# Recurrent attention and a two-layer network: the second layer of nine units by seven half-width products, decay sums in a state bank, new engine orders

## The chip, the cores and the metric

The kernel runs on one core of one Trainium2 chip. The metric is device time in microseconds for one launch; the runs of a kernel are given by their median.

## The reference

A gated recurrent attention is followed by a two-layer network with a squared relu. Shapes: batch 4, 8 heads, 768 tokens, head size 48; model width 8 x 48 = 384, hidden width 2048. All inputs and the output are float32.

```python
for t in range(S):
    state = alpha[:, :, t, :, None] * state + np.einsum('bhd,bhe->bhde', k[:, :, t], v[:, :, t])
    y[:, :, t] = np.einsum('bhd,bhde->bhe', q[:, :, t], state)
...
x = np.ascontiguousarray(attn_out.transpose(0, 2, 1, 3)).reshape(B * S, H * D)
h = x @ w_in
r = np.maximum(h, 0.0)
g = r * r
return (g @ w_out).astype(np.float32)
```

## The kernel before, in words

The 4 x 768 tokens are cut into 12 units of 256 tokens (T), three for each batch entry; unit g belongs to batch entry g mod 4, so a unit's recurrent state is needed four units later. In a unit the tokens are held in pairs, so that a tile of 128 partitions holds 128 token pairs and a free index j of 2.

A unit goes through these steps; the names are those in the order lists, with the unit's number behind them.

- Loads `lda ldk ldq ldv` bring alpha, k, q and v into one of four `raw` tiles, most of them issued on SP.
- Decays: `pr` multiplies alpha over a pair (DVE or POOL), `ln` takes the logarithm (ACT), `m1i` sums it with a triangular matrix on PE into a PSUM bank called W, and ACT reads that bank three times (`ei`, `ea`, `ec`) for the exponentials. From unit 4 on DVE also reads it (`lb`). `bk` (POOL or DVE) multiplies the inverse decays by alpha.
- `ekm` and `eqm` (DVE) scale k and q by the decays; both of their inputs are in SBUF. A DMA transpose `tr` from SP brings them to `kqt`.
- Scores `p0` on PE fill both banks of the PSUM tile psX and both of psZ (banks Z0 and Z1); DVE masks them (`mk0`, `mk1`) into `pm`.
- `y` is a block of small matmuls for the output of unit g. The state matmuls of unit g+1 are in the middle of it and write Z0 and Z1; DVE then does `sa` and `sc`, and `sd` (POOL or DVE) decays the state. `xe` evicts the output, and `xt` transposes it by DMA.
- First layer: eight blocks `s1_g_u` of six matmuls of 256 columns fill banks H0 and H1 in turn. `re` (ACT or DVE) applies the relu into `rr`, and `sq` squares it into the tile `gt` (two buffers): `sq_g_1`, `_3`, `_5` take two blocks (1024 columns), `_6` and `_7` one (512). Squares run on DVE, ACT or POOL, as the order lists say.
- Second layer: for each token parity j, 16 matmuls of 384 columns accumulate in bank O, issued as four quarters `s2_g_j_0` to `_3`. `oe` evicts each half, and `out` stores the unit.

Which engine does what, and in which order, is written out by hand in `ORDERS`, one list per engine; every engine is a strict queue. A `Program` collects the operations with what they read and write, derives the waits, and goes through the lists with a cost for each operation and a rule for POOL and DVE at work together. What comes of this on the chip is only the place of the semaphores and of the filler matmuls at the start; the order itself is given. The last unit's second half is computed in two column cuts of 272 and 112 (`last_tile`), with two evictions and two stores.

## Time and profile before

| what | value |
|---|---|
| runs, median (lowest, highest) | 176.27 us (173.71, 177.86), 3 runs |
| profiled execution | 173.93 us, span 172.2 us, granted clock 1.0 |
| PE busy | 160.9 us, 93% of the span |
| DVE busy | 117.2 us, 68% |
| ACT busy | 104.5 us, 61% |
| POOL busy | 64.6 us, 37% |

The span is the time between the first and last recorded instruction of the profiled execution; its device time is 1.7 us more. Busy time of an engine is the union of its instructions. In the rows of groups the columns are line, engine, operation, output and input tiles with shape, count, then busy time in us, mean time of one in ns, and the idle time before them with what ended it. In the rows of the chain and of the timeline the first two numbers are start and length in us.

### The profile page before, as it was taken

To read this page: it belongs to the slowest core of one execution; us is meant where nothing else is said; L and a number is where in the kernel's file an instruction comes from. 1 tells how busy PE (TensorE), PEld (TensorE's weight loads), DVE (VectorE), ACT (ScalarE), POOL (GpSimd) and SP (SyncE) were. 2 spreads that over 40 slices of the span, in tenths; PEclk is the share of its full clock that TensorE was granted. 3 is DMA by queue.
4 is the path that set the end of the run, shared out by engine and by line. 5 is a ranking of instruction groups with operands and counts; after the bars stand their busy time and mean duration, and the time that the engine had idled before them with its cause. 6 is when DMAs were issued, how large, how long until landed. Compare 5 with 4: busy or idle time off the path is not lost.

```text
span 172.2 us, 5038 instructions
## 1 busy us (share of the span) xinstructions
PE 160.9 (93%) x2200; PEld 127.6 (74%) x2200; DVE 117.2 (68%) x186; ACT 104.5 (61%) x190; POOL 64.6 (37%) x65
## 2 busy tenths in 40 slices
PE   0696999999999999999999999999999999999994
PEld 0564799756788877887877887878777877687773
DVE  4478889768977787769566848799517709355241
ACT  2837478767677866466785578377668454152240
POOL 4947214910286554481640466001012122403700
PEclk9999999999999999999999999999999999999999
DMA  5999999999997999999999999999983672220012
GB/s 139 346 256 244 291 276 212 204 272 297 159 240 183 292 221 179 221 222 251 205 221 293 219 197 243 162 286 317 183 209 115 90 84 93 48 93 0 24 71 91
DMA packets 71559, 33.37 MB, mean 194 GB/s; under 512 B 67568, under 2 KB 68592, under 8 KB 71536
## 3 DMA queue, kind: packets, MB, share of 16 engines
q1 hardware_dynamic: 69024, 26.75, 70.4%
q0 software_dynamic: 2512, 6.29, 15.4%
q8 instruction: 17, 0.28, 0.7%
q14 instruction: 6, 0.05, 0.1%
HBM read 25.17 MB, written 4.72 MB: 174 GB/s over the span
## 4 chain that ended last, share of the span: by engine, by line
PE 90%; DVE 3%; ACT 2%; DMA 2%; issue 1%; DVEq 0%; ACTq 0%
PE psWH L1029 36%; PE psO L1070 33%; PE psX L925 3%; PE psZ L796 2%; PE psX L828 2%; DMA raw<-in_alpha_dram 2%; PE psX L817 2%; PE psWH L1070 2%; PE psX L997 2%; PE psZ L925 1%; PE psWH L669 1%; DVE pm L936 1%; PE psO L1029 1%; PE psX L864 1%; PE psX L971 1%
## 5 line engine op out<-in xcount | busy, mean ns | idle before, releaser
L1029 PE MATMUL psWH<-xt,win 128*128 128x256 bf16 x552 | 71.0, 274 | 0.2 <-ACT rr L1037 0.2
L1070 PE MATMUL psO<-wout,gt 128*128 128x384 bf16 x352 | 66.3, 326 | 0.0
L1029 PEld LDWEIGHTS psWH<-xt,win 128*128 128x128 bf16 x552 | 61.4, 129 | 5.3 <-DVE xt L983 0.6
L1070 PEld LDWEIGHTS psO<-wout,gt 128*128 128x128 bf16 x352 | 33.4, 98 | 17.5 <-DVE gt L1047 0.5
L1037 ACT ACTIVATE rr<-psWH 128x512 bf16<-128x512 f32 x58 | 33.9, 595 | 15.4 <-PE psWH L1029 14.5
L1050 POOL TENSOR_TENSOR gt<-rr 128x1024 bf16<-128x1024 bf16 (+1 forms) x17 | 28.0, 1654 | 37.4 <-ACT rr L1037 20.8
L1039 DVE TENSOR_SCALAR rr<-psWH 128x512 bf16<-128x512 f32 x34 | 23.4, 690 | 19.5 <-PE psWH L1029 19.0
L1051 ACT ACTIVATE gt<-rr 128x512 bf16<-128x512 bf16 (+1 forms) x26 | 21.1, 824 | 5.8 <-DVE rr L1039 5.8
L1077 ACT ACTIVATE osb<-psO 128x384 f32<-128x384 f32 x18 | 8.8, 490 | 17.0 <-PE psO L1070 16.8
L936 DVE TENSOR_TENSOR pm<-psZ,caus 128x1024 bf16<-128x1024 f32 x12 | 14.6, 1220 | 3.1 <-PE psZ L925 3.1
L726 POOL CAST vbf<-raw 128x768 bf16<-128x768 f32 x8 | 6.7, 832 | 24.6 <-DMA raw<-in_v_dram 24.6
L936 DVE TENSOR_TENSOR pm<-psX,caus 128x1024 bf16<-128x1024 f32 x12 | 14.6, 1216 | 0.5 <-PE psZ L925 0.5
L1047 DVE TENSOR_TENSOR gt<-rr 128x1024 bf16<-128x1024 bf16 (+1 forms) x17 | 10.6, 625 | 2.9 <-ACT rr L1037 2.4
L687 POOL TENSOR_TENSOR ek<-ek,raw 128x384 f32<-128x384 f32 x6 | 6.5, 1082 | 15.8 <-ACT ek L680 15.8
L731 DVE TENSOR_TENSOR qks<-raw,eq 128x384 bf16<-128x384 f32 x18 | 9.4, 553 | 2.6 <-DMA raw<-in_q_dram 1.8
L736 DVE TENSOR_TENSOR qks<-raw,ek 128x768 bf16<-128x768 f32 x11 | 10.5, 955 | 0.5 <-POOL ek L687 0.4
L704 DVE TENSOR_TENSOR la<-psWH,la 128x384 f32<-128x384 f32 x8 | 4.4, 553 | 7.9 <-ACT eq L682 6.5
L661 ACT ACTIVATE lab<-prd 128x384 bf16<-128x384 f32 x10 | 5.2, 522 | 4.1 <-POOL prd L660 2.4
L956 ACT ACTIVATE xbf<-psX 128x768 bf16<-128x768 f32 x7 | 5.7, 810 | 3.3 <-PE psX L817 3.0
L660 POOL TENSOR_TENSOR prd<-raw 128x384 f32<-128x384 f32 x5 | 5.2, 1040 | 4.9 <-DMA raw<-in_alpha_dram 4.9
L680 ACT ACTIVATE ek<-psWH 128x384 f32<-128x384 f32 x10 | 4.9, 490 | 3.0 <-PE psWH L672 2.2
L958 DVE CAST xbf<-psX 128x768 bf16<-128x768 f32 x5 | 4.8, 954 | 2.0 <-PE psX L817 1.3
(128 smaller groups left out, 183.7 us busy)
## 6 DMA issues: line engine op xcount, KB each, us to landing
out_dram<-osb SPq DMA_DIRECT2D x11, 384.0 KB, 4.0
raw<-in_alpha_dram SPq DMA_DIRECT2D x10, 384.0 KB, 4.5
raw<-in_k_dram SPq DMA_DIRECT2D x10, 384.0 KB, 4.6
raw<-in_q_dram SPq DMA_DIRECT2D x10, 384.0 KB, 4.8
raw<-in_v_dram SPq DMA_DIRECT2D x10, 384.0 KB, 4.9
wout<-in_moe_w_out_dram POOLq DMA_DIRECT2D x2, 768.0 KB, 8.4
raw<-in_alpha_dram POOLq DMA_DIRECT2D x2, 384.0 KB, 6.5
raw<-in_k_dram POOLq DMA_DIRECT2D x2, 384.0 KB, 7.2
```

The costliest lines, as they stand in the source:

```text
L731: add("dve", lambda e, j=j, dst=dst: e.tensor_tensor(dst, RAW[r][:, 2, :, j, :].rearrange("p (n x) d -> p n x d", x=2), EQ[la][:, j].rearr ...
L736: add("dve", lambda e, a=a, E=E: e.tensor_tensor(QKS[qs][:, a, :, :, 0:D], RAW[r][:, 1 + a].rearrange("p h j d -> p j h d"), E[la][:].rear ...
L925: ins = pe.matmul(psT[64 * c:64 * c + 64, rr_, o:o + 128], keys, mov)
L936: add("dve", lambda e, hf=hf, psT=psT: e.tensor_tensor(PM[pm][:, hf].rearrange("p r n j t -> p (r n) (j t)"), psT[:, :, :].rearrange("p r ...
L1029: ins = pe.matmul(psF[:, i * T:(i + 1) * T], WIN[:, kk, hidden(fj)], mov, start=(kk == 0), stop=(kk == KT - 1))
L1037: add("act", lambda e, psF=psF, rr=rr: e.activation(rr, psF, AF.Relu), act_ns(512), pu + 600, reads=[keyF], writes=[("rr", rb, half)], nam ...
L1039: alts={"dve": (lambda e, psF=psF, rr=rr: e.tensor_scalar(rr, psF, 0.0, None, ALU.max), dve_ns(512))})
L1047: add("dve", lambda e, dst=dst, sq=sq: e.tensor_tensor(dst, sq, sq, ALU.mult), 148 + k * 267, pu + 1200, reads=[("rr", rb, h) for h in ran ...
L1050: alts={"pool": (lambda e, dst=dst, sq=sq: e.tensor_tensor(dst, sq, sq, ALU.mult), 200 + k * 840), "act": (lambda e, dst=dst, sq=sq: e.act ...
L1051: "act": (lambda e, dst=dst, sq=sq: e.activation(dst, sq, AF.Square), act_ns(k * 512))})
L1070: ins = pe.matmul(psS, GT[gt][:, fj, j, :], WOUT[:, fj, :], start=(fj == 0), stop=(fj == FT - 1))
L1077: add("act", lambda e, j=j, psS=psS: e.activation(OSB[ob][:, j], psS, AF.Copy), act_ns(DM), ps_ + 700, reads=[keyS], writes=[("osb", ob, j ...
```

## The change

Units 2 to 10 (`STRASSEN`) compute their second layer by Strassen's scheme with seven products in place of eight. The matrices are split in two in each dimension: the tokens by j, the hidden blocks by parity f, the output columns into halves of 192. A product `s2_g_m1` to `m7` is 8 matmuls of 192 columns, issued as two halves (`m10`, `m11` and so on), so a unit has 56 matmuls of 192 columns where it had 32 of 384. The products use two PSUM banks in turn, O and W.

The weights' four sums are made once, in two halves: `ws0` to `ws3` (POOL or DVE, 768 elements a partition). For each unit and each half of the hidden blocks, three sums of activations are made in SBUF from `gt`: `ga` writes two differences into `SG` (1024 elements a partition), `gb` overwrites one quarter of `gt` (512), `gc` writes `SH` (512). `SG` and `SH` have one buffer each. m6 needs `gb`; m5 and m7 need `SG`; m3 needs `SH`. A unit's two evictions `oe` give way to seven of 192 columns: two copies (`ca`, `cc`, ACT or DVE) and five adds of a PSUM bank and an SBUF tile (`cb`, `cd`, `ce`, `cf`, `cg`, all on DVE).

Since bank W is now an accumulator of the products, the decay sums of units 4 to 11 go to bank Z0, which the scores and the state also use. `decays` becomes a step of its own and, for these units, stands after the output block of unit g-2 and ahead of the scores of unit g-1.

All five order lists are new. In number of operations: ACT 190 to 199, DVE 186 to 243, PE 245 to 299, POOL 61 to 100, SP 80 to 82. Of the new sums, `ga` is 13 times on POOL and 5 on DVE, `gb` 9 and 9, `gc` 10 and 8. Relus go from 62 to 76 on ACT and from 34 to 20 on DVE; squares from 17 to 21 on POOL, from 17 to 14 on DVE, from 26 to 25 on ACT. Two early loads (`lda1`, `ldv1`) go from POOL to SP. The rule for POOL and DVE at work together is left out of the program's costs, and some of its costs are changed.

```diff
-    SBUF_ONLY = ("pr", "bk", "aq", "ekm", "eqm", "sq", "sb", "sd")
-    SWITCH = 95
+    ENTER = {"F": 11, "C": 195, "R": 195, "T": 220}
+    COLD = 9000
...
-                if e == "pool" and o.sem is None or e == "dve" and o.name.startswith(self.SBUF_ONLY):
-                    other = shared["dve" if e == "pool" else "pool"]
-                    o.end += max(0.0, min(other - now, 1200.0)) * (0.8 if e == "dve" else 0.5)
-                    shared[e] = o.end
...
+    EITHER = (1, 2, 3)
+    SUMS, SPLIT = 30000, 2
+    STRASSEN = tuple(range(2, 11))
+    SUM_BANK = {g: "Z0" for g in range(4, G)}
...
+    SW = nc.alloc_sbuf_tensor("sw", [128, 4, FT // 2, DM // 2], BF16)
+    SG = nc.alloc_sbuf_tensor("sg", [128, FT // 2, 2, 128], BF16)
+    SH = nc.alloc_sbuf_tensor("sh", [128, FT // 2, 128], BF16)
...
+            go = lambda e, dst=dst, src=src: e.dma_start(dst, src)
+            load_op[name] = add(ring, go, cost, at,
+                writes=[key], name=f"ld{name}", dma=f"{nm}{r}", lag=1230 if ring == "sp" else 1180,
+                alts={"sp": (go, 600), "pool": (go, 930)} if g in EITHER else None,
...
+        psC, keyC = bank(SUM_BANK.get(g, "W"))
+        psM, keyM = bank(STRICT_BANK.get(g, SUM_BANK.get(g, "W")))
...
+            reads=[("lab", la), ("linc",), ("ones",)], writes=[keyC], name=f"m1i{g}")
...
+    def decays(g):
...
+    def weight_sums(w):
+        us, n = slice(4 * w, 4 * w + 4), DM // 2
+        b11, b12, b21, b22 = (WOUT[:, 8 * w + f:8 * w + 8:2, c * n:c * n + n] for f in range(2) for c in range(2))
+        t1, t2, t3, t4 = (SW[:, k, us] for k in range(4))
+        for k, (dst, x, y, op, src) in enumerate(((t3, b12, b22, ALU.add, ()), (t1, b12, b11, ALU.subtract, ()),
+                                                  (t2, b11, t3, ALU.subtract, (2,)), (t4, t2, b21, ALU.add, (1,)))):
+            add("pool", lambda e, dst=dst, x=x, y=y, op=op: e.tensor_tensor(dst, x, y, op), 90 + 1.86 * 4 * n, SUMS + k,
+                reads=[("wout", w)] + [("sw", q, w) for q in src], writes=[("sw", (2, 0, 1, 3)[k], w)], name=f"ws{k}_{w}",
+                alts={"dve": (lambda e, dst=dst, x=x, y=y, op=op: e.tensor_tensor(dst, x, y, op), dve_ns(4 * n, 2))})
+    def second_layer_strassen(g):
+
+        b, i = units[g]
+        gt, ob, n, nu = g % NGT, g % NOSB, DM // 2, FT // 2
+        p0 = DENSE.get(g, g * P + 20500) + P * 0.5 + 600
+        step = P * 0.5 / 7
+        G4 = GT[gt][:].rearrange("p (u f) j t -> p u f j t", f=2)
+        row = FT * 2 * 128
+
+        def view(us, off, dims):
+            return bass.AP(tensor=GT[gt], offset=us.start * 512 + off, ap=[[row, 128], [512, us.stop - us.start]] + dims)
+
+        cut = nu // SPLIT
+        for x in range(SPLIT):
+            us = slice(x * cut, (x + 1) * cut)
+            r = range(us.start, us.stop)
+            ga = lambda e, us=us: e.tensor_tensor(SG[:, us], view(us, 128, [[0, 2], [1, 128]]),
+                                                  view(us, 0, [[384, 2], [1, 128]]), ALU.subtract)
+            gb = lambda e, us=us: e.tensor_tensor(G4[:, us, 0, 1], SG[:, us, 1], G4[:, us, 0, 0], ALU.subtract)
+            gc = lambda e, us=us: e.tensor_tensor(SH[:, us], G4[:, us, 1, 0], G4[:, us, 0, 1], ALU.add)
+            add("dve", ga, dve_ns(cut * 256, 2), p0 - 1000 + x, alts={"pool": (ga, 90 + 1.86 * cut * 256)},
+                reads=[k for u in r for k in (("gt", gt, 2 * u, 0), ("gt", gt, 2 * u, 1), ("gt", gt, 2 * u + 1, 1))],
+                writes=[("sg", x)], name=f"ga{g}_{x}")
+            add("dve", gb, dve_ns(cut * 128, 2), alts={"pool": (gb, 90 + 1.86 * cut * 128)}, prio=p0 - 900 + x, reads=[("sg", x)] + [("gt", gt, 2 * u, 0) for u in r],
+                writes=[("gt", gt, 2 * u, 1) for u in r], name=f"gb{g}_{x}")
+            add("dve", gc, dve_ns(cut * 128, 2), alts={"pool": (gc, 90 + 1.86 * cut * 128)}, prio=p0 - 800 + x, reads=[("gt", gt, 2 * u + 1, 0) for u in r] + [("gt", gt, 2 * u, 1) for u in r],
+                writes=[("sh", x)], name=f"gc{g}_{x}")
+
+        def phase(k, name, psS, key, left, right, keys, first):
+            for h in range(2):
+                def run(pe, h=h):
+                    for u in range(h * nu // 2, (h + 1) * nu // 2):
+                        ins = pe.matmul(psS, left(u), right(u), start=(first and u == 0), stop=(u == nu - 1),
+                                        skip_group_check=True)
+                    return ins
+                add("pe", run, pe_ns(nu // 2, n), p0 + (k + 0.4 * h) * step, reads=keys(h), writes=[key],
+                    name=f"s2_{g}_{name}{h}")
+
+        (psA, keyA), (psB, keyB) = bank("O"), bank("W")
+        psA, psB = psA[:, 0:n], psB[:, 0:n]
+        o = [[OSB[ob][:, j, c * n:c * n + n] for c in range(2)] for j in range(2)]
+
+        def keys(*parts):
+            def of(h):
+                us = range(h * nu // 2, (h + 1) * nu // 2)
+                k = []
+                for p in parts:
+                    k += ([("gt", gt, 2 * u + p[1], p[2]) for u in us] if p[0] == "gt" else
+                          [(p[0], x) for x in range(h * SPLIT // 2, max(h * SPLIT // 2 + 1, (h + 1) * SPLIT // 2))]
+                          if p[0] in ("sg", "sh") else [p + (h,)])
+                return k
+            return of
+
+        wout = [[lambda u, f=f, c=c: WOUT[:, 2 * u + f, c * n:c * n + n] for c in range(2)] for f in range(2)]
+        sums = [lambda u, t=t: SW[:, t, u] for t in range(4)]
+        gtl = [[lambda u, f=f, j=j: GT[gt][:, 2 * u + f, j, :] for j in range(2)] for f in range(2)]
+        ok = [[("osb", ob, j, c) for c in range(2)] for j in range(2)]
+
+        def copy(k, name, src, key, dst, dkey):
+            add("act", lambda e: e.activation(dst, src, AF.Copy), act_ns(n), p0 + k * step, reads=[key], writes=[dkey],
+                name=f"{name}{g}", alts={"dve": (lambda e: e.tensor_copy(dst, src), dve_ns(n))})
+
+        def plus(k, name, src, key, x, xkey, dst, dkey):
+            add("dve", lambda e: e.tensor_tensor(dst, src, x, ALU.add), dve_ns(n), p0 + k * step, reads=[key, xkey],
+                writes=[dkey], name=f"{name}{g}")
+
+        phase(0, "m1", psA, keyA, gtl[0][0], wout[0][0], keys(("gt", 0, 0), ("wout",)), True)
+        copy(0.5, "ca", psA, keyA, o[1][0], ok[1][0])
+        phase(1, "m6", psB, keyB, gtl[0][1], sums[1], keys(("gt", 0, 1), ("sw", 1)), True)
+        plus(1.5, "cb", psB, keyB, o[1][0], ok[1][0], o[0][1], ok[0][1])
+        phase(2, "m2", psA, keyA, gtl[1][0], wout[1][0], keys(("gt", 1, 0), ("wout",)), False)
+        copy(2.5, "cc", psA, keyA, o[0][0], ok[0][0])
+        phase(3, "m7", psB, keyB, lambda u: SG[:, u, 0], sums[2], keys(("sg",), ("sw", 2)), False)
+        plus(3.5, "cd", psB, keyB, o[1][0], ok[1][0], o[1][1], ok[1][1])
+        phase(4, "m5", psA, keyA, lambda u: SG[:, u, 1], sums[0], keys(("sg",), ("sw", 0)), True)
+        plus(4.5, "ce", psA, keyA, o[1][1], ok[1][1], o[1][1], ok[1][1])
+        phase(5, "m4", psB, keyB, gtl[1][1], sums[3], keys(("gt", 1, 1), ("sw", 3)), False)
+        plus(5.5, "cf", psB, keyB, o[1][0], ok[1][0], o[1][0], ok[1][0])
+        phase(6, "m3", psA, keyA, lambda u: SH[:, u], wout[1][1], keys(("sh",), ("wout",)), False)
+        plus(6.5, "cg", psA, keyA, o[0][1], ok[0][1], o[0][1], ok[0][1])
+        dst = out[b * S + i * T:b * S + i * T + T, :].rearrange("(p j) n -> p (j n)", j=2)
+        add("sp", lambda e, dst=dst: e.dma_start(dst, OSB[ob][:].rearrange("p j n -> p (j n)")), 600, p0 + 7 * step,
+            reads=[("osb", ob, 0), ("osb", ob, 1)], name=f"out{g}_1", dma=f"o{ob}", lag=1150)
...
-    ORDER = ["f0", "k0", "p0", "f1", "y0", "p1", "k1", "y1", "f2", "p2", "k2", "s0", "s1"]
+    ORDER = ["f0", "k0", "p0", "d1", "f1", "y0", "p1", "k1", "y1", "t0", "t1", "d2", "f2", "p2", "k2", "s0", "s1"]
-        ORDER += [f"f{g}", f"w{g - 1}", f"p{g}"]
+        ORDER += [f"w{g - 1}"] if g in SUM_BANK else [f"d{g}", f"f{g}", f"w{g - 1}"]
+        ORDER += [f"d{g + 1}"] * (g + 1 in SUM_BANK) + [f"p{g}"] + [f"f{g + 1}"] * (g + 1 in SUM_BANK)
```

The new POOL list from the cast of unit 2 on, the old one from the same place, and the new DVE and PE lists over one unit's length:

```
new POOL: vc2 sq0_5 sq0_7 sd1 ws1_0 bk3 vc3 sd2 pr4 ws1_1 vc4 ws2_1 pr5 sd3 ga2_0 gb2_0 bk5 sq2_7 ga2_1 sq3_1 sd4 sq3_3
sq3_5 bk6 ga3_0 ga3_1 gb3_1 gc3_0 sd5 sq4_3 bk7 sq4_5 ga4_0 ga4_1 gb4_1 gc4_0 sq5_1 bk8 gc4_1 ga5_0 gb5_0 sd7
vc8 pr9 ga5_1 gc5_1 sq6_1 gc5_0 ga6_0 gb6_0 pr10 sq7_1 gc6_0 sd6 sq7_5 sq7_6 vc10 gc6_1 pr11 ga7_0 gb7_1 bk11
gc7_1 ga8_0 gb8_0 vc11 gc8_1 sq9_1 sq10_1 ga9_0 gb9_1 sq10_5 sq10_7 ga10_1 gb10_0 sq11_3 gc10_0 sq11_5 sq11_7

old POOL: vc2 sd2 bk4 sq2_1 pr5 vc4 sd3 bk5 sq2_7 sq3_1 sd4 pr6 sq3_7 sq3_6 vc6 sd5 pr7 sq4_3 bk7 vc7 pr8 sq5_1 bk8 vc8
pr9 sq6_3 bk9 sq6_6 sq6_5 vc10 bk11 vc11 sq9_3 sq9_7 sq10_1 sq10_6 sq11_1 sq11_3

new DVE: ekm8 eqm1_8 eqm0_8 mk1_7 cf4 cg4 sq5_6 mk0_7 sq5_7 re6_2 sq6_3 sa8 re6_4 gb5_1 bk9 lb9 cb5 ekm9

new PE: m1i8 s2_4_m50 s2_4_m70 s2_4_m71 s2_4_m51 s1_5_5 s1_5_6 s2_4_m40 s1_5_7 p0_7 s2_4_m30 s2_4_m41 s2_4_m31 s1_6_1
s1_6_0 s2_5_m60 s1_6_3 s1_6_2 y7 s2_5_m10 s1_6_4 s2_5_m11 m1i9
```

163 lines of the change are left out of this document (89 added, 74 removed).

## The prediction

> **What bounds the kernel now.** I read the page first: busy shares, the span in slices, the chain that ended last.
>
> ```profile
> span 172.2 us, 5038 instructions
> PE 160.9 (93%) x2200; PEld 127.6 (74%) x2200; DVE 117.2 (68%) x186; ACT 104.5 (61%) x190; POOL 64.6 (37%) x65
> PE   0696999999999999999999999999999999999994
> PE 90%; DVE 3%; ACT 2%; DMA 2%; issue 1%; DVEq 0%; ACTq 0%
> ```
>
> From the fifth slice on PE is full, and it holds 90% of the chain: today time is PE work. Next the chain in order of time, for the price of PE work, and the groups by shape for the last tile.
>
> ```profile
> 58.97 1.31 PE psWH L1029 x12
> 60.28 1.30 PE psO L1070 x8
> ...
> 62.62 1.47 PE psWH L1029 x12
> ...
> 68.91 0.35 PE psX L925 x16
> 69.26 0.22 PE psZ L925 x16
> ...
> 122.86 0.27 PE psWH L669
> ...
> 167.23 2.65 PE psX L997 x32
> 169.91 0.27 DVE osl L1004
> 170.18 0.27 DVEq L338
> ...
> L997 PE MATMUL psX<-wout,gt 128*128 128x272 bf16 x16 | 2.0, 279 | 0.0
> L997 PE MATMUL psX<-wout,gt 128*128 128x112 bf16 x16 | 1.0, 213 | 0.0
> L1070 PEld LDWEIGHTS psO<-wout,gt 128*128 128x128 bf16 x352 | 33.4, 98 | 17.5 <-DVE gt L1047 0.5
> ```
>
> Eight second-layer matmuls of 384 columns take 1.30 us, 162.5 ns each; twelve of 256 take 1.31 us, 109.2 each: 53.3 ns for 128 columns, so 0.4164 ns a column and 2.6 fixed. The last tile tests it: 16 of 272 and 16 of 112 should take 16 x (115.9 + 49.2) = 2.64 us; they took 2.65. So the line holds down to 112 columns with a full weight load for each, and the 98 ns shown per load is not its spacing.
>
> **The change on PE.** A unit's 32 matmuls of 384 columns (5.20 us) become 56 of 192, at 2.6 + 192 x 0.4164 = 82.5 ns: 4.62 us. Nine units save 9 x 0.58 = **5.2 us**. From below the row is the 112-column one (49 ns, overall time per column already used); from above, 98 ns a load would make it 5.49 us, a loss of 0.29 x 9 = 2.6 us. I take 82.5, between two shapes that fit one line.
> The Trainium skill (TensorE: Matmul & The Clock Gate, LDWEIGHTS) gives a load of 128 columns as 128/1.2 = 107 ns; by an estimate from that figure 56 loads would be 6.0 us, and the nine units would lose 7 us. The trace disagrees: 32 loads and matmuls fit in 2.65 us.
>
> **What the change puts on the other engines.** I take the stretch from the decay sum of unit 5 to that of unit 11, and then the rest.
>
> ```profile
> 52.50:122.90 70.40, 70.06 (x1066) 56.42 (x1065) 55.39 (x83) 47.25 (x87) 27.56 (x24) 1.00 1.08 234
> 122.90:169.90 47.00, 46.91 (x505) 36.63 (x503) 21.36 (x31) 22.18 (x38) 11.58 (x8) 1.00 0.37 87
> ```
>
> Columns after the length: PE, PEld, DVE, ACT, POOL. PE is full in both, POOL has 27.6 of 70.4 us. The new POOL order gives it, from bk5 up to bk11, 45 operations in place of 23: nine ga, nine squares of 1024 and two of 512, twelve gb and gc, four bk, three pr, four sd, two vc. Prices: ga has the squares' form (1024 bf16 out of two bf16 inputs), gb and gc that of 512.
>
> ```profile
> L1050 POOL TENSOR_TENSOR gt<-rr x17: 1038/1892/2568, 29.5 to 161.5; 128x1024 bf16<-128x1024 bf16 x11, 128x512 bf16<-128x512 bf16 x6
> 84.23 1.00 POOL L660 TENSOR_TENSOR prd<-raw 128x384 f32<-128x384 f32 x1 [1.56 <-DMA raw<-in_alpha_dram]
> 88.34 1.00 POOL L687 TENSOR_TENSOR ek<-ek,raw 128x384 f32<-128x384 f32 x1 [1.26 <-ACT ek L680]
> L726 POOL CAST vbf<-raw 128x768 bf16<-128x768 f32 x4 | 3.3, 822 | 19.8 <-DMA raw<-in_v_dram 19.8
> L900 POOL TENSOR_TENSOR sbd<-tmp,acm 128x384 bf16<-128x384 f32 x3 | 2.5, 829 | 0.0
> ```
>
> 18 x 1.89 + 14 x 1.04 + 7 x 1.00 + 4 x 0.83 + 2 x 0.82 = **60.5 us**. PE in that stretch gets 47 first-layer blocks for 46, 70 half products (4 matmuls, 0.33 us) for 40 quarters (0.65 us), and one output block less (from 60.28 + 1.30 to 62.62 in the chain, 1.0 us): 70.4 + 0.66 + 23.1 - 26.0 - 1.0 = **67.2 us**. Taken alone POOL would fit, at 90%.
>
> It isn't alone. Here are POOL operations and DVE's beside them, by start and duration:
>
> ```profile
> 29.33 0.95 DVE L736 TENSOR_TENSOR qks<-raw,eq 128x768 bf16<-128x768 f32 x1
> 29.47 2.57 POOL L1050 TENSOR_TENSOR gt<-rr 128x1024 bf16<-128x1024 bf16 x1 [1.88 <-ACT rr L1037]
> ...
> 53.06 0.69 DVE L1047 TENSOR_TENSOR gt<-rr 128x1024 bf16<-128x1024 bf16 x1
> 53.14 1.48 POOL L687 TENSOR_TENSOR ek<-ek,raw 128x384 f32<-128x384 f32 x1 [0.48 <-ACT ek L680]
> ...
> 74.80 0.68 DVE L1047 TENSOR_TENSOR gt<-rr 128x1024 bf16<-128x1024 bf16 x1
> 74.97 2.27 POOL L1050 TENSOR_TENSOR gt<-rr 128x1024 bf16<-128x1024 bf16 x1 [0.30 <-DVE rr L1039]
> ...
> 58.84 1.89 POOL L1050 TENSOR_TENSOR gt<-rr 128x1024 bf16<-128x1024 bf16 x1 [2.12 <-ACT rr L1037]
> 59.96 1.21 DVE L936 TENSOR_TENSOR pm<-psX,caus 128x1024 bf16<-128x1024 f32 x1
> ```
>
> Where DVE is inside an operation with both inputs in SBUF, POOL's is longer: 0.68 us for an overlap of 0.81, 0.48 for 0.61, 0.38 for 0.51, that is the overlap less 0.13. It does nothing until DVE lets go. With one DVE input in PSUM (the last pair) both run freely. And of the 64 DVE operations with two SBUF inputs, none starts inside a POOL operation. So the two kinds exclude each other, and their times add.
> The Trainium skill (SBUF — State Buffer, Who interferes with whom) states it as a lock held for the whole instruction, against which the loser fully blocks, for GpSimd reads and DVE operations with two SBUF inputs. The trace agrees on POOL's side with the 0.38 to 0.68 us above; no row shows DVE held back, so which engine pays is open, but the sum is the same.
>
> DVE's operations of that kind in the stretch (from ekm5 up to ekm11) go from 32 to 45: six ekm, twelve eqm, six of 1024 (four squares, two ga), fifteen of 512 (five squares, ten gb and gc), three pr, two bk and one weight sum.
>
> ```profile
> L736 DVE TENSOR_TENSOR qks<-raw,ek 128x768 bf16<-128x768 f32 x6 | 5.7, 955 | 0.5 <-POOL ek L687 0.4
> L731 DVE TENSOR_TENSOR qks<-raw,eq 128x384 bf16<-128x384 f32 x12 | 6.1, 552 | 1.8 <-DMA raw<-in_q_dram 1.8
> L1047 DVE TENSOR_TENSOR gt<-rr 128x1024 bf16<-128x1024 bf16 x8 | 5.5, 688 | 0.2
> L1047 DVE TENSOR_TENSOR gt<-rr 128x512 bf16<-128x512 bf16 x1 | 0.4, 415 | 0.0
> ```
>
> 6 x 0.955 + 18 x 0.552 (the pr, bk and the sum priced as eqm) + 6 x 0.688 + 15 x 0.415 = 26.0 us; less 0.13 each, 20.2. **POOL and these together: 80.7 us, where PE has 67.2.** Before, the like sum was 27.6 + 20.9 (32 operations) = 48.5 of 70.4, which fitted.
>
> So PE must wait about 13.5 us, less what POOL may run late before PE notices. At the stretch's end bk11 is followed by gc7_1, which the last half product of unit 7 (m31) waits for; PE has 12 half products, 4 first-layer blocks and one score block (0.35 + 0.22) ahead of it, 4.0 + 2.6 + 0.6 = 7.2 us after the decay sum, and POOL needs some 3.5 after it (1.0 for bk11, 1.04 for gc7_1, the rest an estimate for the exponential ahead, 0.5 us and its handovers): 4 us of slack. That leaves 9.5. Nor will two strict queues hand over without holes: DVE's evictions stand behind a held operation and PE behind them, and POOL's ga waits for the single SG buffer until m5 and m7 of the unit before. I put 5% on 80.7, 4 us. **Port term: +13.5 us**, between +1 (all lateness carried past unit 11: there 18 POOL and 16 such DVE operations, 25.3 + 6.5 us at the same prices, meet 44.6 us of PE, which is 47.0 with 56 halves and 4 quarters in place of 34 quarters and two first-layer blocks less; 112.5 against 111.8 in all) and +28 (15% holes, no slack).
>
> **The remaining edits.** Each unit's two output evictions become two copies and five adds of 192 columns.
>
> ```profile
> L891 DVE TENSOR_TENSOR smd<-psZ,sbd 128x384 bf16<-128x384 f32 x6 | 3.3, 552 | 0.5 <-PE psX L817 0.5
> L1039 DVE TENSOR_SCALAR rr<-psWH 128x512 bf16<-128x512 f32 x34 | 23.4, 690 | 19.5 <-PE psWH L1029 19.0
> L1004 DVE COPY osl<-psX 128x112 f32<-128x112 f32 x1 | 0.3, 274 | 3.6 <-PE psX L997 3.6
> L1077 ACT ACTIVATE osb<-psO 128x384 f32<-128x384 f32 x18 | 8.8, 490 | 17.0 <-PE psO L1070 16.8
> ```
>
> An add is 274 + 80 x 278/272 = 356 ns, one input in PSUM, so it excludes nothing; 45 of them are 16 us of DVE, while 14 relus (690 ns each) and 6 large squares go to other engines; by the counts of both orders at such prices DVE ends near 133 us busy, ACT near 110. Those fit if DVE isn't held. They release two alternating PSUM accumulators (O and W), where a product waits for the eviction two products back. The new order puts about 1 us of other PE work between; a release needs 0.36 us, its start after PE and the wake of PE. Between 0 and +3, taken +0.5.
> Decay sums in Z0 must wait for sa, and the next scores behind them for four readers; 3.6 us of PE work lies between m1i8 and p0_7, so free unless DVE is late: 0 to +2, taken +0.3.
> Three weight sums on POOL and five on DVE fall in units 1 to 5, where POOL and such DVE work still fit: 0. lda1 and ldv1 go behind unit 0's loads on SP, where they delay lda3 by two issues, and leave POOL's queue earlier for the weights; ln1 moves ahead: -0.7 to +1, taken 0. At the end out10 is issued about 3 us before PE's last matmul; no row prices its overlap with the three final stores, so 0 to +1, taken 0.
> Sum: 173.9 (profiled execution: span 172.2 and 1.7 around it) - 5.2 + 13.5 + 0.8 = 183.0. The median of the three runs is 2.3 above that execution, with runs on both sides; I add half: **184 us**.
>
> **Rivals.**
> *PE stays the bound* (faster): the exclusion costs nothing because either side runs ahead enough. For it: PE shows 70.06 of 70.40 now in spite of several such meetings. Against: 80.7 does not go into 67.2, and POOL's work can't start before its squares. 183.0 - 13.5 = 169.5, with the half 171. It wins if POOL and DVE turn out to share after all. Chance 0.15.
> *The lateness is carried* into the last units, where POOL and DVE have 44.6 - 31.8 = 13 us free: +2 to +6 in place of +13.5, so 173 to 177. Against: 4 us of slack counted. Chance 0.13.
> *Accumulators as a new wait*: if evictions, queued behind DVE's held operations, come late for every product, 63 times 0.3 us adds 19 to the sum without the port term: 188 to 190. Chance 0.08.
> *The products save nothing* (98 ns a load is the spacing) and the port doesn't bind: 173.9 + 2.6 + 1.2 = 177.7. Chance 0.02, since L997's row speaks against it.
>
> **How the numbers follow.** Forecast 184 with chance 0.62; its own range 178 to 190. The full range, 170 to 192, takes in the carried lateness and most of the first rival, and leaves about 0.15 outside. A measurement of this kernel tells about 2%, 3.5 us, from no change: faster is the first rival (0.15), no change the second and fourth (0.15), slower the forecast and the third (0.70).
>
> **What would show it.** Right: PE's slices from the 13th to the 30th drop to 7 or 8; POOL is near full there, with squares and ga well above 1.89 us in the mean; the 192-column products still show 0.33 us for four where nothing holds them; the chain gains DVE and POOL shares. Wrong: POOL's means stay at 1.9 and 1.04 while DVE's two-input operations start inside them; or PE's slices stay at 9 and the span falls by 5 us; or PE waits chiefly for the adds that empty O and W.

## The result and the profile after

The changed kernel takes **201.5 us** in the median (199.92 to 204.59, 4 runs) against 175.25 us for the kernel before in 4 runs on the same chip: a ratio of 1.150, 95% interval 1.134 to 1.167. The forecast was 184, the range 170 to 192. Medians are over all runs; ratios and intervals leave out runs in a slower state (of the four, the one at 204.59). The profiled execution took 201.31 us, with a span of 199.5.

The page after: span, busy shares, PE, DVE, POOL and the granted clock in 40 slices, and the chain that ended last.

```profile
span 199.5 us, 5682 instructions
PE 170.6 (86%) x2453; PEld 142.8 (72%) x2453; DVE 172.2 (86%) x243; ACT 108.9 (55%) x199; POOL 138.8 (70%) x104
PE   7999988989769959698799469799879799797995
DVE  4488998999999997999999999989998957969531
POOL 3837669399277976878799948999967361866560
PEclk9999999999996996999999999999999999999999
DVE 49%; PE 38%; ACT 4%; issue 3%; POOL 3%; DMA 2%; SPq 0%; DVEq 0%
```

PE is no longer full from the 12th slice on; DVE is, with hardly a break from the 9th to the 32nd, and it holds half of the chain, where PE held 90%. DVE's busy time rose by 55 us. The groups by shape say what with (columns as before: count, busy us, mean ns, idle before).

```profile
L750 DVE TENSOR_TENSOR qks<-raw,eq 128x384 bf16<-128x384 f32 x18 | 26.7, 1508 | 0.9 <-DMA raw<-in_q_dram 0.4 <-ACT eq L699 0.3
L755 DVE TENSOR_TENSOR qks<-raw,ek 128x768 bf16<-128x768 f32 x11 | 16.3, 1484 | 0.0
L1101 DVE TENSOR_TENSOR sh<-gt 128x512 bf16<-128x512 bf16 x8 | 8.0, 1016 | 0.0
L1098 DVE TENSOR_TENSOR sg<-gt 128x1024 bf16<-128x1024 bf16 x5 | 7.0, 1395 | 0.0
L1066 DVE TENSOR_TENSOR gt<-rr 128x1024 bf16<-128x1024 bf16 x7 | 7.7, 1106 | 0.2 <-ACT rr L1056 0.2
L1145 DVE TENSOR_TENSOR osb<-psWH,osb 128x192 f32<-128x192 f32 x27 | 9.4, 349 | 3.9 <-PE psWH L1114 3.8
L955 DVE TENSOR_TENSOR pm<-psX,caus 128x1024 bf16<-128x1024 f32 x12 | 14.6, 1215 | 1.0 <-PE psX L944 0.5 <-PE psZ L944 0.4
L1069 POOL TENSOR_TENSOR gt<-rr 128x1024 bf16<-128x1024 bf16 x16 | 34.1, 2136 | 11.2 <-DVE rr L1058 8.7 <-ACT rr L1056 2.5
L1098 POOL TENSOR_TENSOR sg<-gt 128x1024 bf16<-128x1024 bf16 x13 | 30.7, 2358 | 6.0 <-ACT gt L1070 3.2 <-PE psO L1114 1.4 <-DVE gt L1066 1.3
L1101 POOL TENSOR_TENSOR sh<-gt 128x512 bf16<-128x512 bf16 x10 | 12.7, 1268 | 6.9 <-DVE gt L1100 6.9
L1100 POOL TENSOR_TENSOR gt<-sg,gt 128x512 bf16<-128x512 bf16 x9 | 11.2, 1241 | 2.7 <-DVE sg L1098 2.2
```

DVE's operations with both inputs in SBUF have grown: `eqm` (L750) from 552 to 1508 ns, `ekm` (L755) from 955 to 1484, the large square from 688 to 1106. Those with an input in PSUM have not: the adds take 349 ns (priced at 356), the masks 1215 (1216 before). The timeline shows why (start, length):

```profile
79.65 2.63 POOL L1098 TENSOR_TENSOR sg<-gt 128x1024 bf16<-128x1024 bf16 x1 [0.90 <-ACT gt L1070]
80.22 3.91 DVE L750 TENSOR_TENSOR qks<-raw,eq 128x384 bf16<-128x384 f32 x2
82.36 1.35 POOL L1100 TENSOR_TENSOR gt<-sg,gt 128x512 bf16<-128x512 bf16 x1
170.84 2.31 POOL L1098 TENSOR_TENSOR sg<-gt 128x1024 bf16<-128x1024 bf16 x1
171.19 2.50 DVE L1098 TENSOR_TENSOR sg<-gt 128x1024 bf16<-128x1024 bf16 x1
```

At 171.19 DVE begins a `ga`, 0.69 us of work (the square's mean before), behind POOL's, which ends at 173.15; DVE's ends at 173.69, 0.54 us after. It was counted as busy for 2.50 us and did nothing for 1.8. Two `eqm`, 1.1 us of work, take 3.91 us beside two POOL sums in a row. So the prediction's open question, which engine pays, has an answer here: mostly DVE, though POOL's records grow too (its large squares from 1.99 to 2.14 us in the mean), and a held DVE instruction looks like a long one, not like an idle engine.

PE's longest waits (in all, times, longest):

```profile
PE psZ L686 <- DVE smd L910: 6.3, 4, 2.2
PE psWH L1114 <- DVE osb L1145: 4.2, 5, 1.8
PE psWH L1114 <- POOL vbf L745: 2.9, 1, 2.9
PE psO L1114 <- DVE osb L1145: 2.3, 2, 1.3
```

Whatever DVE does reaches PE late: `sa` (L910), behind which the decay sum in Z0 waits, and the adds that empty O and W. These are short operations in a queue of held ones. The third row belongs there too, as I read it: an add on DVE ends 0.06 us before that wait does, and the weight load beside it is put down to the add.

I take the prediction's stretches, from the decay sum of unit 5 to that of unit 11 and from there to the end (columns after the length: PE, PEld, DVE, ACT, POOL):

```profile
59.90:147.10 87.20, 72.18 (x1138) 64.52 (x1138) 84.98 (x106) 51.43 (x98) 71.67 (x45) 0.96 0.83 176
147.10:199.50 52.40, 45.84 (x597) 41.17 (x597) 36.77 (x63) 21.44 (x35) 27.69 (x18) 1.00 0.32 85
```

| part | before | after | change | predicted |
|---|---|---|---|---|
| start to decay sum of unit 5 | 52.1 | 59.9 | +7.8 | 0 |
| to decay sum of unit 11 | 70.7 | 87.2 | +16.5 | +10.3 |
| to the end | 49.4 | 52.4 | +3.0 | -2.4 |

(The predicted middle is PE's saving there, 67.2 - 70.4, and the port term of 13.5; 0.8 us of other terms and 1.2 of offset were not put to a part. The marks are the starts of the two decay sums, one profiled execution on each side.)

### The profile page after: what moved, and what is told of

Same layout as the page of the kernel before. It is cut to its first block, busy times and chain, and to the rows that moved or that the text cites. A ratio compares the mean times of both kernels' runs of the same rounds, so it can differ in the third digit from the quotient of the medians.

```text
span 199.5 us, 5682 instructions
## 1 busy us (share of the span) xinstructions
PE 170.6 (86%) x2453; PEld 142.8 (72%) x2453; DVE 172.2 (86%) x243; ACT 108.9 (55%) x199; POOL 138.8 (70%) x104
## 4 chain that ended last, share of the span: by engine, by line
DVE 49%; PE 38%; ACT 4%; issue 3%; POOL 3%; DMA 2%; SPq 0%; DVEq 0%
DVE qks L750 11%; PE psWH L1048 10%; DVE pm L955 7%; DVE qks L755 6%; PE psO L1114 6%; PE psWH L1114 4%; PE psO L1248 4%; PE psO L1186 3%; DVE osb L1145 3%; DVE sh L1101 3%; DVE gt L1066 3%; DVE sg L1098 3%; DVE prd L674 2%; DMA raw<-in_q_dram 2%; DVE gt L1100 2%
## 5 line engine op out<-in xcount | busy, mean ns | idle before, releaser
L1069 POOL TENSOR_TENSOR gt<-rr 128x1024 bf16<-128x1024 bf16 (+1 forms) x21 | 39.6, 1890 | 13.3 <-DVE rr L1058 10.9
L1098 POOL TENSOR_TENSOR sg<-gt 128x1024 bf16<-128x1024 bf16 x13 | 30.7, 2358 | 6.0 <-ACT gt L1070 3.2
L750 DVE TENSOR_TENSOR qks<-raw,eq 128x384 bf16<-128x384 f32 x18 | 26.7, 1508 | 0.9 <-DMA raw<-in_q_dram 0.4
L1114 PE MATMUL psWH<-sw,gt 128*128 128x192 bf16 x144 | 17.0, 249 | 7.8 <-DVE osb L1145 4.2
L1070 ACT ACTIVATE gt<-rr 128x1024 bf16<-128x1024 bf16 (+1 forms) x25 | 21.0, 849 | 0.3
L1114 PEld LDWEIGHTS psWH<-sw,gt 128*128 128x128 bf16 x144 | 11.9, 98 | 10.4 <-DVE osb L1145 8.6
L1114 PE MATMUL psO<-wout,gt 128*128 128x192 bf16 x144 | 16.3, 250 | 2.3 <-DVE osb L1145 1.3
L1101 POOL TENSOR_TENSOR sh<-gt 128x512 bf16<-128x512 bf16 x10 | 12.7, 1268 | 6.9 <-DVE gt L1100 6.9
L755 DVE TENSOR_TENSOR qks<-raw,ek 128x768 bf16<-128x768 f32 x11 | 16.3, 1484 | 0.0
L955 DVE TENSOR_TENSOR pm<-psX,caus 128x1024 bf16<-128x1024 f32 x12 | 14.6, 1215 | 1.0 <-PE psX L944 0.5
L1114 PEld LDWEIGHTS psO<-wout,gt 128*128 128x128 bf16 x144 | 12.0, 99 | 3.6 <-DVE osb L1145 1.7
L1186 PE MATMUL psO<-wout,gt 128*128 128x384 bf16 x64 | 12.1, 326 | 0.0
```

Of the source, the lines that this page charges most:

```text
L750: add("dve", lambda e, j=j, dst=dst: e.tensor_tensor(dst, RAW[r][:, 2, :, j, :].rearrange("p (n x) d -> p n x d", x=2), EQ[la][:, j].rearr ...
L755: add("dve", lambda e, a=a, E=E: e.tensor_tensor(QKS[qs][:, a, :, :, 0:D], RAW[r][:, 1 + a].rearrange("p h j d -> p j h d"), E[la][:].rear ...
L955: add("dve", lambda e, hf=hf, psT=psT: e.tensor_tensor(PM[pm][:, hf].rearrange("p r n j t -> p (r n) (j t)"), psT[:, :, :].rearrange("p r ...
L1069: alts={"pool": (lambda e, dst=dst, sq=sq: e.tensor_tensor(dst, sq, sq, ALU.mult), 200 + k * 840), "act": (lambda e, dst=dst, sq=sq: e.act ...
L1070: "act": (lambda e, dst=dst, sq=sq: e.activation(dst, sq, AF.Square), act_ns(k * 512))})
L1098: ga = lambda e, us=us: e.tensor_tensor(SG[:, us], view(us, 128, [[0, 2], [1, 128]]), view(us, 0, [[384, 2], [1, 128]]), ALU.subtract)
```

## Experiments

Three theories stood at the start. The first: POOL's reads of SBUF and DVE's two-input operations exclude each other, and that is the cost. The second: DVE's own added work is the cost. The third: the handovers of PSUM banks (O, W, Z0) are. Each kernel ran beside the kernel before on the same chip; where a ratio is given its time is the median of at least four runs, elsewhere the time of a single run.

**Take POOL's reads away, keep its work.** POOL's 32 sums become fills of the same tiles; the sums' values are left out.

```diff
-alts={"pool": (ga, 90 + 1.86 * cut * 256)}
+alts={"pool": (lambda e, us=us: e.memset(SG[:, us], 0.0), 90 + 1.86 * cut * 256)}
 ... (gb and gc alike)
```

> The 32 sums of activations that the changed kernel has on POOL (13 ga, 9 gb, 10 gc) are replaced by memsets of the same output, so POOL only writes there and reads nothing from SBUF; the 22 sums on DVE and all orders stay, and the sums' values are left out of the product. Theory 1 (DVE operations with two SBUF inputs are held inside the instruction while POOL reads SBUF, 45 us of holds in all, and DVE is a full queue, so holds set the time): eqm, from 1.51 us in the mean, comes down to 0.7 to 1.0 and the time to 176 to 184 us. Theory 2 (DVE is full from the operations that it got, 45 adds and 22 sums, whatever POOL does): DVE's operations are all there, so 197 to 203 us. Theory 3 (the decay sums in bank Z0 hold PE): 197 to 203 us, PE's wait for sa stays at 6 us.

Measured 181.58 us, before 174.71, in the first theory's range. Twenty of the 26 us go with the reads of 32 instructions:

```profile
L750 DVE TENSOR_TENSOR qks<-raw,eq 128x384 bf16<-128x384 f32 x18 | 12.8, 738 | 2.5 <-DMA raw<-in_q_dram 1.8 <-ACT rr L1056 0.3 <-ACT eq L699 0.3
```
```profile
PE 166.1 (92%) x2450; PEld 141.7 (79%) x2453; DVE 147.8 (82%) x243; ACT 108.2 (60%) x199; POOL 104.5 (58%) x104
```

The first row is the group of `eqm`, the second the page. `eqm` falls to 738 ns and DVE's busy time by 24 us with not one DVE instruction changed. But a fill is also shorter (0.95 us for 2.36), so this alone does not separate the reads from POOL's time. The 7 us that remain above the kernel before are not separated here.

**Add POOL's reads to the kernel before.** In two kernels POOL gets 32 extra operations (13 of 1024 elements, 19 of 512) into a scratch tile, at places like those of the sums: once sums that read SBUF, once fills.

```diff
+e.tensor_tensor(junk, win, win, ALU.add)     # first kernel
+e.memset(junk, 0.0)                          # second kernel
```

> The kernel before, nothing of it changed, with 32 operations added on POOL alone, as many and as large as the changed kernel's sums there (13 of 1024, 19 of 512 elements, two bf16 inputs from a weight tile, output to a scratch tile that nobody reads), placed around the second layer of units 2 to 10. PE, ACT and DVE have the same work as before. Theory 1: DVE's operations with two SBUF inputs are held, and the time rises to 184 to 194 us with qks operations well above 0.553 and 0.955 us. Theories 2 and 3: POOL was 37% busy and has room, so 174 to 179 us, the rise only from POOL's own queue.

> The same 32 added operations on POOL as memsets of the scratch tile, which read nothing. Theory 1: 174 to 178 us, DVE's durations as before. If POOL's queue itself is what hurts, as much as with the reading form.

Measured 190.8 us with the reads and 176.09 with the fills, before 174.91. `eqm` in the first and in the second:

```profile
L735 DVE TENSOR_TENSOR qks<-raw,eq 128x384 bf16<-128x384 f32 x18 | 19.0, 1080 | 1.3 <-ACT eq L710 0.7 <-DMA raw<-in_q_dram 0.4
```
```profile
L735 DVE TENSOR_TENSOR qks<-raw,eq 128x384 bf16<-128x384 f32 x18 | 10.0, 581 | 1.2 <-ACT eq L710 0.8 <-DMA raw<-in_q_dram 0.2
```

With PE's, ACT's and DVE's lists as before, POOL's sums cost 15.9 us and the fills 1.2, which lies within the spread of the kernel before there (173.90 to 176.09). 53 us of POOL time against 22 may be a part of that difference, but a wait for a late POOL result shows as idle time ahead of a DVE instruction (0.4 us ahead of `ekm` before the change), not in its length: DVE's 581 ns beside POOL's fills and 1080 beside its sums is the exclusion seen by itself. The Trainium skill (SBUF — State Buffer, Who interferes with whom) says that a DVE instruction with two SBUF inputs contends with a GpSimd instruction that reads SBUF, not with one that only writes it; these two runs agree.

**Move POOL's sums to DVE.** All 32 sums go to DVE, at the places where they were due; DVE gets 17 us more of work.

```diff
 pool: ... pr5 sd3 -ga2_0 -gb2_0 bk5 sq2_7 -ga2_1 sq3_1 ...
 dve:  ... mk1_3 +ga2_0 ws3_1 sq2_5 sa4 +gb2_0 sc4 ... eqm0_5 +ga2_1 eqm1_5 ...
```

> The 32 sums on POOL move to DVE, each at the place in DVE's list that its turn on POOL had in time; nothing is left out. DVE gets 13 x 0.69 + 19 x 0.42 = 17 us of own work and POOL loses 57 us. Theory 1: the holds caused by these 32 go, some 25 of 45 us, more than the 17 us put on DVE: 188 to 196 us. Theory 2: DVE was full with its own work, 17 us more make 212 to 220 us. Theory 3: no change from this, 199 to 204 us apart from DVE's part.

Measured 189.27 us: 12 us faster than after, with more work on the engine that looked full. DVE's busy time is 164.8 us, less than after's 172.2. So not all of its 172 were work, and the second theory as it stood falls.

**Move DVE's adds to ACT.** The 45 adds become copies on ACT, with the addition left out; DVE loses 16 us of work that takes no part in the exclusion.

```diff
-add("dve", lambda e: e.tensor_tensor(dst, src, x, ALU.add), ...)
+add("act", lambda e: e.activation(dst, src, AF.Copy), ...)
```

> The 45 adds that evict products go from DVE to ACT as plain copies of the PSUM bank (the addition of the other term is left out, ACT has no two-tensor add here). DVE loses 45 x 0.35 = 16 us that need no second SBUF input; ACT, 55% busy, gets 15 us. Theory 2 (DVE's own work is the bound): 184 to 188 us. The prediction's own form of theory 1 (the sum of POOL's operations and DVE's two-input ones is the bound, and other DVE work fits beside): nothing of that sum changes, 198 to 202 us. Theory 1 as the profile now suggests (DVE full with own work plus holds): a part of the 16 us comes back as longer holds, 188 to 196 us.

Measured 199.52 us. `eqm` rises to 1646 ns, and between the decay sums of units 5 and 11 the kernel needs 88.5 us:

```profile
L754 DVE TENSOR_TENSOR qks<-raw,eq 128x384 bf16<-128x384 f32 x18 | 29.1, 1646 | 2.5 <-DMA raw<-in_q_dram 2.1 <-ACT eq L703 0.3
```
```profile
59.50:148.00 88.50, 72.38 (x1138) 64.69 (x1138) 80.09 (x82) 57.52 (x123) 70.74 (x45) 0.94 0.81 172
```

What DVE was spared came back as longer holds and as idle time. That fits the prediction's form, in which the sum of POOL's and DVE's excluding work sets the pace in that order and not DVE's load.

**Leave the weight sums out.** The eight weight sums become fills, in the changed kernel.

```diff
-add("pool", lambda e, dst=dst, x=x, y=y, op=op: e.tensor_tensor(dst, x, y, op), ...
+add("pool", lambda e, dst=dst: e.memset(dst, 0.0), ...
 ... (on DVE alike)
```

> The changed kernel with its eight weight sums replaced by memsets of the same tiles (three on POOL, five on DVE), so that they read nothing; their values are left out. The changed kernel reaches the decay sum of unit 5 at 59.9 us, 7.8 us later than before. Theory 1 (POOL and DVE already exclude each other there, and the weight sums are the new work in it): 54 to 57 us at that mark and 194 to 198 us in all. Rival for this stretch (the new places of loads and first steps): 59 to 60 us, and 199 to 203 us.

Measured 200.78 us. The decay sum of unit 5 comes at 55.6 in place of 59.9, as expected, but that of unit 11 at 146.6 in place of 147.1: the 4.3 us won are taken back in the middle, which now needs 91.0 us. Its expectation for the total was missed. An early gain was worth nothing here, with a later stretch as the bound.

**Put the decay sums in Z0, alone.** The kernel before, with the decay sums of units 4 to 11 in Z0 and the few entries moved that this asks for (among them the sums of units 5 and 11, two score blocks, a relu, a square). It is built by the changed kernel's program, so the new costs and the new order of its steps came with it.

```diff
+SUM_BANK = {g: "Z0" for g in range(4, G)}
-... s1_2_5 m1i5 y3 s1_2_6 s1_2_7 ...
+... s1_2_5 y3 s1_2_6 m1i5 s1_2_7 ...
```

> The kernel before with one part of the change: the decay sums of units 4 to 11 go to bank Z0 (no products of half width, no sums, no adds). Its orders are the old ones but for ten places on PE and four elsewhere that the bank asks for. Theory 3 (Z0 and its readers cost a good part of the 27 us): 182 us or more, with PE waiting for sa. Theories 1 and 2: Z0 costs little where DVE isn't late, 174 to 179 us.

Measured 179.99 us (4 runs), ratio 1.028 (1.021 to 1.035): between the expectations. 2.7 us of it arise before Z0 is used: the decay sum of unit 2, still in W, starts at 28.16 against 25.48. From there on this kernel needs 3.4 us more than before. So the edit costs some 2 to 3 us from where Z0 is used, not 0.3; PE's waits for `sa` are 1.0 us of that, the rest is not separated from the moved entries. The start's share came with the edit and has no cause that I showed.

**Other orders for the same work.** The next kernels have engines and orders chosen so that POOL's reads and DVE's two-input operations seldom meet. In the first, with all of the change's work, POOL keeps 2 of its 13 `ga` and 7 of 21 squares, and ACT takes 41 squares:

```
POOL: ... vc2 sq1_7 sd2 sq1_6 vc4 sd3 bk4 pr5 sd4 bk5 gc2_1 vc5 pr6 gc2_0 bk6 gb3_0 gb3_1 vc6 sd5 bk7 sq4_6 ga4_1 gc4_1 bk8 ...
```

> All of the change's work with other order lists and other choices of engine, searched so that POOL's operations and DVE's with two SBUF inputs seldom meet: POOL keeps 2 of its 13 ga and 7 of its 21 squares; DVE has 16 ga and ACT 41 squares in place of 25; the adds and the bank Z0 stay as in the change, nothing is left out. Theory 1: without the holds the saving on PE shows, 168 to 175 us. Theory 2: DVE has 21 operations more than in the change, so 200 us or more. Theory 3: Z0 and its readers are the same, at least 190 us.

Measured 182.51 us, ratio 1.049 (1.039 to 1.058), a miss for all three theories. The holds are gone (`eqm` 600 ns), but DMA now has 17% of the chain:

```profile
51.19 5.95 DMA kqt<-qks
57.16 4.77 DMA raw<-in_q_dram
```

Transposes and the load of q behind them had been packed too late, as I read these rows. The second choice leaves them room (POOL: 2 `ga`, 9 `gb`, 11 `gc`, 11 squares). With it ran two kernels whose orders were chosen in the same way: one with the products in units 8 to 10 only, and, as a control, one with the work of the kernel before. The second choice's POOL list:

```
POOL: ... vc2 sd2 bk4 pr5 ga2_0 gb2_0 gc2_0 bk5 vc5 gc2_1 sd4 sq3_1 bk6 gb3_1 pr7 bk7 gc4_0 sq4_6 pr8 gb4_1 gc4_1 vc8 sq5_7 gc5_1 bk9 ...
```

> All of the change's work (seven products in units 2 to 10, decay sums of units 4 to 11 in bank Z0, 8 weight sums), with orders in which POOL reads SBUF seldom beside DVE's two-SBUF-input operations and in which the waits for transposes and loads have more room than in e6_order_for_exclusion: POOL has 2 of the 18 ga, all 9 and 11 of the gb and gc, 11 squares; DVE has 16 ga, 9 gb, 7 gc, 12 squares. Theory 1 (the exclusion was the price; what e6 lost beside it were late landings): 172 to 178 us, eqm at 0.55 to 0.65 us, little DMA in the chain. Theory 2 (with a second unit of work on DVE and ACT and a shared bank Z0, PE waits for handovers in any order): 180 to 186 us. Theory 3 (the products gain once the orders fit): below 171 us.

> Seven products in units 8 to 10 only (3 x 0.58 = 1.7 us less of PE work), decay sums of units 10 and 11 alone in Z0, weight sums spread over the middle, orders chosen so that POOL's reads and DVE's two-SBUF-input operations seldom meet. Theory 1: with 6 ga, 9 gb and gc and little else added, the span is that of before less 1.7 to plus 1: 172 to 176 us. Theory 2 (the handovers cost in proportion to the units): 176 to 179 us. Against e11_before_other_orders, the same search of orders without the products, theory 1 gives -2 to 0 us and theory 2 +1 to +4 us.

> The kernel before with its own work unchanged and only its orders and engines chosen in the same way as in e9_full_second_order and e10_last_three_units: what that choice does by itself. Nothing of the change is in it. PE bounds it in both theories: 173 to 178 us; above 178 would say that the way of choosing costs time by itself, and e9 and e10 have to be read against this kernel rather than against before.

Measured 178.56 us, ratio 1.019 (1.013 to 1.025); 177.27 us, 1.011 (1.006 to 1.017); 176.17 us, 1.007 (1.004 to 1.011); before 174.88. The full change gets 23 us faster than as delivered, just outside the first theory's range; the second of the three came out in the second theory's; the control as expected, so the way of choosing costs some 1.3 us by itself.

The rest of the first one's loss has two parts. Its weight sums lie in the chain ahead of unit 5, five on DVE with 3.2 us, so they were left out again (fills in their place):

> e9_full_second_order with its 8 weight sums left out: each (0.55 to 0.95 us on DVE, 1.80 us on POOL) is a memset of the same tile (estimate from e5_no_weight_sums: 0.38 us on DVE, 0.74 us on POOL), everything else and all orders the same. Theory 1 (the weight sums stand in the chain before unit 5, where e9's chain has 3.2 us of them on DVE): the decay sum of unit 5 starts 1.5 to 2.5 us earlier than e9's 57.2, and what is gained stays: 175.5 to 177.2 us. Theory 2 (PE is late there through the handovers over bank Z0 whatever DVE does): within 0.8 us of e9, 177.8 to 179.4 us.

Measured 176.37 us, ratio 1.004 (1.000 to 1.009): from 1.019, some 2.6 us less, as the first theory had it; the decay sum of unit 5 comes at 55.0 in place of 57.2, and this time the gain stays. And ACT loaded its table three times at the start, all in the chain, since its list had the load in fifth place:

```profile
4.24 1.28 ACT L579
6.49 1.28 ACT L600
8.67 1.28 ACT L466
```

```diff
-ln0_0 ln1_0 ei0_0 ei1_0 table ea0_0 ea1_0 ...
+table ln0_0 ln1_0 ei0_0 ei1_0 ea0_0 ea1_0 ...
```

> e9_full_second_order with one entry moved: the load of ACT's table stands first in ACT's list, as before and after the change, where e9 has it fifth. In e9's trace ACT loads a table three times at the start, 1.28 us each, all three in its chain (at 4.24, 6.49 and 8.67 us); with the table first it is loaded once, ahead of the first input. Theory 1 (these loads are a part of e9's remaining 3.7 us, and the handovers of the change the smaller part): 2.5 to 4 us off, 174.5 to 176.5 us, which is the time of before within 1%. Theory 2 (the start's gain is taken back by the first full stretch of DVE, as in e5_no_weight_sums): less than 1 us off, 177.6 to 179 us. Faster than before, below 173 us, by none of the theories.

> e10_last_three_units with ACT's table load first in its list (e10 loads it in between, two more loads of 1.28 us in its chain at 4.29 and 6.54 us). In e10 the decay sum of unit 2 starts 4.6 us later than before the change, and from there to the end it needs 145.7 us against 146.7. Theory 1 (the start's delay goes, PE bounds the rest): 172.5 to 174.5 us, that is 0 to 1.5% faster than before. Theory 2 (the delay is taken up elsewhere anyway): 176 to 178 us.

Measured 176.38 us, ratio 1.007 (1.003 to 1.011), at the upper end of the first theory's range, with 2.1 us off by the ratios where 2.5 to 4 was expected; and 176.38 us, 1.006 (1.003 to 1.010), in the second theory's range: PE alone would have given 172.5 to 174.5. Neither is faster than before, and no version that I ran is. The stretches of the full change in this order, from the decay sum of unit 5 to that of unit 11 and to the end:

```profile
55.00:127.50 72.50, 69.28 (x1152) 63.42 (x1151) 70.17 (x123) 56.50 (x104) 32.87 (x31) 1.00 1.11 220
127.50:174.40 46.90, 44.46 (x593) 41.17 (x591) 29.49 (x60) 24.62 (x39) 19.45 (x14) 1.00 0.41 96
```

POOL is down from 71.7 to 32.9 us; the end is 2.5 us shorter than before, by the half products; the middle is 1.8 us longer, where PE's work alone would make it 3.2 shorter. DVE is busy there for 70.2 of 72.5 us, with `eqm` at 552 ns: now it is its own work that fills it. That DVE's load is what keeps the middle above PE's 67.2 us is my reading of that row; no run took DVE's load away in this order. PE's waits of 3.0 us there are all for DVE (1.6 for adds, 0.9 for `sa`, 0.5 for a `gb`), which the handovers of the banks by themselves would show too; and PE's own busy time is 69.3 us where 67.2 was counted, which stays open.

## Why the prediction was right and wrong

The mechanism held and the sum failed. By the table above, the middle came out 6.2 us over its forecast, the start 7.8 and the end 5.4, less the 2.0 us that were put to no part. The port term was mis-sized, and the same exclusion was put at nothing in the stretches ahead of it and behind it.

**PE's price: right.** Four matmuls of 192 columns were to take 0.33 us, eight 0.66. The chain after:

```profile
118.38 0.34 PE psO L1114 x4
120.72 0.66 PE psO L1114 x8
121.38 0.34 PE psWH L1114 x4
```

The saving of 5.2 us is real work saved; where nothing holds PE it shows (the last stretch of the good order, -2.5 us where -2.4 was counted). The Trainium skill (TensorE: Matmul & The Clock Gate, LDWEIGHTS) gives a weight load by a formula that makes 107 ns of 128 columns. Taken as the spacing of the products, by which the units would have lost 7 us, it does not describe them: four, with a load each, take 0.34 us.

**The mechanism: right.** Forecast in kind (POOL and DVE's two-input work add up, PE waits) and in sign. "What would show it" came true: PE's slices from the 13th to the 30th fell to 7.7 in the mean, POOL's `ga` and squares went above 1.89 us, the chain gained DVE. POOL is busy for 82% of the middle, less than the "near full" that was expected. And one sign of being wrong, "PE waits chiefly for the adds", came half true: the adds are PE's largest wait (6.5 us, 9.4 with the one put down to POOL's cast), `sa` the next (6.3). The rival that the two share after all, at 0.15, falls: 32 POOL sums cost the kernel before 15.9 us, 32 fills 1.2. (Of the 64 DVE operations said never to start inside a POOL operation one does, 0.05 us before its end; that changes nothing.)

**The port term: right in form, too small.** It was 13.5 us in the stretch; 87.2 - 67.2 makes it 20.0. Three of its figures were off:

1. The prices. `ga` took the squares' 1.89 us, `gb` and `gc` their 1.04. Unhindered, POOL's `ga` takes 2.13 us and `gb` and `gc` 1.16. That the sums read `gt` in pieces of 128 is not the reason: the sums added to the kernel before read whole runs and take as long (third row). The squares multiply a tile by itself, the sums take two different inputs and another operation; no run separates these. With nine `ga` and twelve `gb` and `gc`, POOL's 60.5 becomes 64.1, and the port's sum 84.3: +3.6.

```profile
76.62 2.13 POOL L1098 TENSOR_TENSOR sg<-gt 128x1024 bf16<-128x1024 bf16 x1
173.77 1.16 POOL L1100 TENSOR_TENSOR gt<-sg,gt 128x512 bf16<-128x512 bf16 x1 [0.62 <-DVE sg L1098]
120.36 2.12 POOL L1064 TENSOR_TENSOR junk<-win 128x1024 bf16<-128x1024 bf16 x1
```

2. The slack. 4 us were taken off because POOL may run late before PE notices at unit 11. But the stretch also began late, and lateness that is there at its start is no credit at its end, as I read it. +4.
3. The holes. 84.3 of 87.2 us would be a port 97% taken; I had put 5% on top, it comes to 3%: -1.

3.6 + 4 - 1 is the missing 6.5 us, by arithmetic of my own on measured rows. The trace allows another split: laid side by side, its records show a POOL operation or a DVE operation of that kind under way for 80.4 of the 87.2 us, which is the forecast's 80.7, and leaves 6.8 us of holes where 4 was put. Common to both is that the slack of 4 us was not granted. PE's clock was also halved twice in this stretch, for 3.4 us each (last section); what that cost here is not separated.

The bounds were off too. The +28 for "15% holes, no slack" should be 80.7 x 1.15 - 67.2 = 25.6, and with that alone the sum is 195, above the 192 at which the range ended.

**The early units: priced at 0, measured +7.8.** "Three weight sums on POOL and five on DVE fall in units 1 to 5, where POOL and such DVE work still fit: 0." They did not: the weight sums are worth 4.3 us at the mark. I had priced them by count against a whole stretch; but POOL's take 1.96 us each and hold DVE. Nor did I count POOL's first two activation sums, which fall ahead of the mark:

```profile
55.29 2.13 POOL L1098 TENSOR_TENSOR sg<-gt 128x1024 bf16<-128x1024 bf16 x1
55.67 2.16 DVE L1080 TENSOR_TENSOR sw<-sw,wout 128x768 bf16<-128x768 bf16 x1
57.50 1.35 POOL L1100 TENSOR_TENSOR gt<-sg,gt 128x512 bf16<-128x512 bf16 x1
57.76 1.63 DVE L1066 TENSOR_TENSOR gt<-rr 128x1024 bf16<-128x1024 bf16 x1
59.92 0.34 PE L686 MATMUL psZ<-lab,linc 128*128 128x384 bf16 x1 [2.02 <-DVE smd L910]
```

A weight sum of 0.55 us and a square of 0.69, which take 3.8 us beside `ga2_0` and `gb2_0`, stand ahead of `sa`, and the decay sum in Z0 waits for that. With POOL's activation sums as fills (the first experiment) the mark comes at 57.0, 2.9 us earlier. So the two kinds of sums, each taken away by itself, are worth 4.3 and 2.9 of the 7.8 us; no run took away both. A further 0.4 is PE work that the new order puts ahead of the mark (5.2 saved less 3.2 and 2.4).

**Z0: 0.3 with an upper bound of 2, 2 to 3 us for the edit that puts it in alone.** In the changed kernel the condition in the text, "free unless DVE is late", is the one that failed: 6.3 us of PE's waits are for `sa`.

**The last units: -2.4, measured +3.0.** The second rival gave them 13 us of room on POOL and DVE. As delivered they still hold each other (the two `ga` at 171 us), and PE waits for adds (at 156.17 for 0.9 us). In the good order they give 2.5 back.

**Accumulators as a new wait** was a rival of its own at 0.08 with 188 to 190 us. It came true as a part of the forecast's mechanism: PE waits 6.5 us for adds, which stand in DVE's queue behind held operations. I had bounded the forecast's sum as if the rivals excluded each other. Early units, port and late units all missed to the same side, as they would with one cause, the holds seen in all three; the upper end of 192 treated them as independent.

**How much is the change's own.** In the order as delivered it costs 26 us. In the best order I found, the same work costs 1.1 us, 176.38 against 175.32, a ratio of 1.007, and 1.007 is also what that way of choosing orders gives for the work of before. So nearly all of the 26 us belong to which engine gets the sums, and when. Of the 5.2 us that PE saves, nothing is left in either.

## What to carry to other kernels

Work given to an engine with room is not free if its operations and those of a busy engine exclude each other: add up the two engines' excluding work over the stretch and compare the sum, not each engine, with the bound. An instruction can be held inside its own duration, so compare the mean duration of each group with its shortest before calling an engine full. When one cause delays several terms of a sum, their bounds add up instead of averaging out.
